# Where the transfers, measures and hashes of the first pairs stand, and a weight chunk behind stores, in a hashed attention followed by a feed-forward block

## The chip, the cores and the metric

The kernel runs on one core of a Trainium2 chip. The metric is the device time of one execution in microseconds, as the median of several executions; lower is better. The core has five instruction streams that run side by side and wait for each other by semaphores: TensorE (PE, matmuls), VectorE (DVE), ScalarE (ACT), GpSimd (POOL) and SyncE (SP, which here only issues DMA transfers). Each of them works through its own instructions in order. ScalarE also issues some transfers; an issue that waits holds up what stands behind it on ScalarE.

## The reference: what is computed

Attention in which a query sees only the keys in its hash bucket, then a two-layer block with a sigmoid gate. q, k and v have the shape (4, 8, 768, 64).

```python
q_bits = (np.einsum('bhsd,dk->bhsk', q, proj) > 0)
k_bits = (np.einsum('bhsd,dk->bhsk', k, proj) > 0)
mask = q_bucket[:, :, :, None] == k_bucket[:, :, None, :]
scores = np.where(mask, scale * np.matmul(q, k.transpose(0, 1, 3, 2)), -1e9)
attn = softmax(scores)
x = np.matmul(attn, v)                # to (3072, 512)
h = x @ w_in                          # 512 x 2048
g = h * (1.0 / (1.0 + np.exp(-1.702 * h)))
out = g @ w_out                       # 2048 x 512
```

## The kernel before, in words

**Pairs.** The 4 x 8 heads are worked through two at a time, as 16 pairs (`pairs`, pair 0 to pair 15). The two heads of a pair fill the 128 partitions. The order of instructions on the four computing engines is the order of the program text (`manual_schedule`, `ORDERED`); SyncE's transfers keep the order of the program through `load`. Nothing here is put in order by a planner.

**What a pair needs.** `fetch(n, "k")` and `fetch(n, "q")` issue four transfers each on SyncE and bring k and q in blocks of 32; `turn` transposes them on VectorE into the tile `own`; `exchange` copies `own` to `other` with the 32-row halves swapped (four transfers on SyncE). `measure` sums the squares of k or q on ScalarE (for a guard at the end; the result isn't used before then), and it reads the tile that `fetch` wrote, as `turn` does. That tile is shared: `fetch(2, name)` writes where pair 0's was, `fetch(3, name)` where pair 1's was, and each waits for the `turn` and the `measure` of the earlier pair. `fetch_v` brings v in one transfer.

**Features.** `hashed(n, at)` multiplies with the hash vectors on TensorE into a PSUM tile; `featured(n)` makes of it signed 0/1 features `f` on VectorE (one instruction) and then spreads `f` over the tile `feats[n % 2]` with eight small transfers of 16 rows (12 KB each). They go out on SyncE, except for two of pair 1 (q, first half), which ScalarE issues. From pair 2 on, `copied` makes a second copy of the features with two more transfers, since `scores_of_four` works on 32-row blocks. The features add a large number to the score where buckets agree, so they stand in the same PSUM sum as the product of q and k; scores of a pair can't begin without them.

**A pair's stream.** `scores` or `scores_of_four` fills PSUM tiles with scores for 128 keys; `weigh` takes the exponential on ScalarE into `es[0]` or `es[1]` (first and second half of the queries). `values` multiplies with v, and `unload` brings the result to `xT` on ScalarE. `add_low` (GpSimd) and `add_high` (VectorE) add the exponentials over the keys; `total` finishes these sums over partitions on TensorE, `invert` and `norm` turn them on VectorE into a factor and scale `xT` by it. In the loop over n = 2 to 15 the second half of pair n-1 and the first half of pair n go side by side, with `invert` and `norm` of pair n-2.

**PSUM tiles.** There are four places of two banks each. `in_turn()` gives them out one after the other by the counter `turns`; a tile waits until the one four turns before it in the same place has been read. Pair 0 takes its places from the written list `slots` and from `place(3)`.

**The row of transfers.** Every transfer of SyncE or ScalarE gets one of eight semaphores, in turn, along one row that the framework lays out; it waits until the transfer eight places before it in the row has landed. So a transfer's place in the row decides whom it waits for, also across the two issuers. `behind_issue(dma, other)` puts a transfer behind another one in the row without making it wait for it.

**Feed-forward.** Weights come in chunks of 512 KB (`convert`: one transfer, then six steps on VectorE and one on ScalarE). The two last chunks of w_in (`late`) are converted after the attention by `conversions`; the first is issued on SyncE right after `hidden(0, 0)`, the first output block, and its first step on VectorE stands in `hidden(0, 1)`. The products use a scheme with seven products in place of eight, nested: `sums_a` and `sums_b` make sums of operands, for a good part on GpSimd (lines 217 to 228), and `keep` stores the gated results to `g_dram`, 256 KB at a time at first; GpSimd's sums of results (`outer_sums`, `g_outer`) overwrite tiles that `keep` is storing, and wait for that.

Of the kernel before, what the change touches and what calls it, by code (L numbers as in the profile page):

```python
# [38 lines left out]
def kernel(  # L39
# [113 lines left out]


# [134 lines left out]
    def attention(ff):  # L289
# [4 lines left out]
        with actx:  # L294
# [47 lines left out]
            def behind_issue(dma, other):  # L342

                tc.add_manual_dep(dma.ins, other.ins.name,
                                  mybir.DependencyInfo(mybir.DependencyClass.NoSync, mybir.DependencyReason.DATA), reason="row")

# [26 lines left out]
            def first_pair():  # L373
# [48 lines left out]
                placed("q", tq, 1, (act, dve))  # L422

# [12 lines left out]
            def exchange(n):  # L436

                for j in range(2):
                    for i in range(2):
                        r0, r1 = D * j + 32 * i, D * j + 32 * (1 - i)  # L440
                        load(other[n % 3][r0 : r0 + 32], own[n % 3][r1 : r1 + 32])
# [19 lines left out]
            def featured(n):  # L461
# [3 lines left out]
                for c in range(2):  # L465
                    for i, x in enumerate("kq"):

                        for j in range(2):
                            r0 = D * i + 32 * c + 16 * j
                            to, of = feats[n % 2][x][D * j : D * j + 16, c * HS : (c + 1) * HS], f[r0 : r0 + 16, :]  # L470
                            if (n, x, c) == (1, "q", 0):
                                nc.scalar.dma_start(out=to, in_=of)
# [143 lines left out]
            fetch_v(0)  # L616
            slots = [2, 0, 1] * 5
            scores(0, 0, low, slots)
            measure(0, "k")
            fetch(2, "k")  # L620
# [10 lines left out]
            fetch_v(1)  # L631
# [5 lines left out]
            values(0, 0, high, at[:, 0])  # L637
            hashed(1, at[:, 1])
            unload(0, 0)
            whole(featured(1))  # L640
            scores(0, 1, high, slots)
# [3 lines left out]
            exchange(2)  # L645
# [24 lines left out]
            next(inverse[0])  # L670
            scores_of_four(1, ((1, 0), (1, 2), (1, 4)))
            add_low(1, 1)
            norm(0)
            add_high(1, 0, (2,))
            for x in "kq":
                measure(3, x)
            at = in_turn()
            values(1, 0, every, at[:, 0])
            hashed(3, at[:, 1])
            unload(1, 0)  # L680
            for n in range(2, last + 1):

                more = n + 2 <= last
                if n == last:

                    turns[0] += 1
# [828 lines left out]
```

## Time and profile before

| | |
|---|---|
| three runs | 859.0, 858.53, 859.93 us (median 859.0) |
| the profiled execution | 857.87 us; span from first to last instruction 856.1 us |
| mean granted TensorE clock | 0.996 |
| TensorE / weight loads | 98% / 61% busy |
| VectorE / ScalarE / GpSimd | 79% / 39% / 43% busy |
| moved by DMA | 144.92 MB, mean 169 GB/s |

How to read the lines: a timeline row has the start and the duration in us, the engine, the line of the kernel, the operation and its tiles (written <- read), how many such instructions are merged, and in square brackets how long the engine had been idle before and who released it. SPq and ACTq are the issuing of transfers by SyncE and ScalarE; the duration there holds the waits between merged issues. A row of a stretch gives the stretch, its length, then busy time and count of TensorE, its weight loads, VectorE, ScalarE and GpSimd, then the granted TensorE clock, the mean busy share of the DMA engines and GB/s. A row of waits gives the total in us, the number and the longest.

### The profile page before, as it was taken

The page shows a single profiled execution, that of the slowest core. Times are in us where ns is not written, and L with a number is a line of the kernel's source. Part 1 is how long each engine was busy: PE and PEld are TensorE (multiplying, and loading weights), DVE is VectorE, ACT ScalarE, POOL GpSimd, SP SyncE. Part 2 cuts the span into 40 slices and gives each one's busy share as a digit, 9 for nine tenths or more (in the row PEclk, how much of TensorE's full clock was granted, in tenths as well). Part 3 has the DMA queues.
Part 4 walks back from the last instruction along what each step waited for, and adds up shares of the span by engine and source line. Part 5 has one row for each costly group of instructions (what it writes and reads, how often), then busy time and mean ns, then how long its engine had stood idle before and what let it go on. Part 6 is the DMA issues. An engine that isn't in the chain of part 4 may idle for free.

```text
span 856.1 us, 14954 instructions
## 1 busy us (share of the span) xinstructions
PE 841.2 (98%) x5644; PEld 522.2 (61%) x5644; DVE 672.1 (79%) x1068; ACT 337.5 (39%) x552; POOL 364.8 (43%) x321
## 2 busy tenths in 40 slices
PE   9989999999999999999999999999999999999996
PEld 4534444444444444565666666545888888888885
DVE  5558788888878986787887788676998977897776
ACT  6746667667666544333444444433000000000000
POOL 4314334434343438997854466668664100000000
PEclk9999999999999999999999999999999999999999
DMA  8476767676674204435566636577854675467524
GB/s 146 86 152 148 153 150 158 129 148 150 143 159 105 72 1 136 159 115 230 198 221 221 221 148 230 187 259 279 286 167 156 205 248 190 162 211 243 191 109 100
DMA packets 165197, 144.92 MB, mean 169 GB/s; under 512 B 124224, under 2 KB 139712, under 8 KB 159872
## 3 DMA queue, kind: packets, MB, share of 16 engines
q1 hardware_dynamic: 154640, 112.11, 46.9%
q10 hardware_dynamic: 10480, 31.81, 11.1%
q8 instruction: 45, 0.74, 0.3%
q14 instruction: 32, 0.26, 0.1%
HBM read 79.69 MB, written 50.33 MB: 152 GB/s over the span
## 4 chain that ended last, share of the span: by engine, by line
PE 87%; POOL 6%; DVE 2%; ACT 1%; issue 1%; DMA 1%; SPq 0%; ACTq 0%; DVEq 0%; POOLq 0%
PE product L1238 30%; PE product L911 16%; PE s L512 15%; PE s L545 14%; PE small L979 5%; PE product L979 2%; PE s L494 2%; PE s L458 1%; PE s L567 1%; ACT e L482 1%; DMA g_dram<-u 1%; POOL c L227 1%; POOL v L226 1%; POOL u L225 1%; POOL w_in_sb L218 0%
## 5 line engine op out<-in xcount | busy, mean ns | idle before, releaser
L482 ACT ACTIVATE e<-s 128x768 f32<-128x768 f32 x192 | 143.3, 812 | 55.8 <-PE s L512 49.1
L545 PE MATMUL s<-e,v 128*32 128x385 f32 x1536 | 131.1, 488 | 0.0
L523 POOL TENSOR_TENSOR t_x<-e 128x768 f32<-128x768 f32 x32 | 59.2, 1849 | 145.6 <-ACT e L482 145.6
L911 PE MATMUL product<-xT,w_in_sb 128*128 128x512 f32 x216 | 100.0, 593 | 0.1
L545 PEld LDWEIGHTS s<-e,v 128*32 128x32 f32 x1536 | 46.6, 109 | 79.3 <-issue 62.0
L911 PE MATMUL product<-t_x,s_in 128*128 128x512 f32 x192 | 89.5, 593 | 1.3 <-ACT u L1033 1.3
L512 PE MATMUL s<-s_in 32*128 32x384 f32 x912 | 89.3, 488 | 0.0
L523 POOL TENSOR_TENSOR t_x<-t_x,e 128x768 f32<-128x768 f32 x32 | 54.6, 1705 | 43.8 <-ACT e L482 42.4
L1274 ACT COPY u<-product 128x256 f32<-128x256 f32 x20 | 7.4, 372 | 158.1 <-PE product L1238 124.9
L536 DVE TENSOR_TENSOR acc<-acc,e 128x768 f32<-128x768 f32 x63 | 67.8, 1076 | 2.1
L911 PEld LDWEIGHTS product<-xT,w_in_sb 128*128 128x128 f32 x216 | 40.9, 190 | 35.8 <-issue 32.7
L512 PEld LDWEIGHTS s<-s_in 32*128 32x128 f32 x912 | 44.8, 187 | 23.7 <-issue 2.9
L911 PEld LDWEIGHTS product<-t_x,s_in 128*128 128x128 f32 x192 | 36.4, 190 | 31.3 <-issue 27.3
L512 PE MATMUL s<-own 32*128 32x384 f32 x432 | 44.3, 482 | 0.0
L463 DVE TENSOR_SCALAR f<-s,above,weight 128x384 bf16<-128x384 f32 x15 | 10.1, 676 | 41.5 <-PE s L567 30.3
L927 DVE TENSOR_TENSOR u<-product,u 128x256 f32<-128x256 f32 (+1 forms) x60 | 28.3, 485 | 15.6 <-PE product L979 12.9
L533 DVE SCALAR_TENSOR_TENSOR acc<-t_x,e 128x768 f32<-128x768 f32 x31 | 29.3, 947 | 11.4 <-POOL t_x L523 10.8
L1238 PE MATMUL product<-raw_g,xT 128*128 128x256 f32 x152 | 35.1, 379 | 0.0
L512 PE MATMUL s<-feat 32*128 32x384 bf16 x336 | 29.8, 327 | 3.8 <-DMA feat<-feat 3.3
L512 PEld LDWEIGHTS <-feat 32*128 32x128 bf16 x336 | 10.3, 92 | 38.1 <-issue 26.2
L225 POOL TENSOR_TENSOR u<-v,u 128x1024 f32<-128x1024 f32 (+1 forms) x11 | 23.8, 2168 | 22.4 <-ACT v L924 14.5
L226 POOL TENSOR_TENSOR v<-c,v 128x1024 f32<-128x1024 f32 (+1 forms) x15 | 32.4, 2158 | 1.0
(297 smaller groups left out, 1781.0 us busy)
## 6 DMA issues: line engine op xcount, KB each, us to landing
raw_g<-g_dram SPq DMA_DIRECT2D x20, 1024.0 KB, 5.1
s_in<-g_dram SPq DMA_DIRECT2D x20, 1024.0 KB, 5.1
g_dram<-c ACTq DMA_DIRECT2D x18, 512.0 KB, 2.9
raw<-in_moe_w_out_dram ACTq DMA_DIRECT2D x16, 512.0 KB, 3.6
raw<-in_moe_w_in_dram ACTq DMA_DIRECT2D x15, 512.0 KB, 3.8
s_in<-own SPq DMA_DIRECT2D x36, 192.0 KB, 4.0
v<-in_v_dram SPq DMA_DIRECT2D x16, 384.0 KB, 4.0
k<-in_k_dram SPq DMA_DIRECT2D x52, 96.0 KB, 3.0
```

Of the source, the lines that this page charges most:

```text
L225: return [lambda: eng.tensor_tensor(t1, b12, b11, op=Alu.subtract), lambda: eng.tensor_tensor(b12, b22, b12, op=Alu.subtract), lambda: eng ...
L226: lambda: eng.tensor_tensor(b12, b22, b12, op=Alu.subtract),
L482: nc.scalar.activation(es[c][:, kt, :, 0:HS], ps[:, :, 0:HS], Act.Exp, scale=1.0 / D**0.5)
L512: nc.tensor.matmul(ps[i][:, j, 0:HS], a[r0 : r0 + 32, keys], m[r0 : r0 + 32, cols], start=at == 0, stop=at == 2)
L523: nc.gpsimd.tensor_tensor(low_sum, low_sum if i else e[:, 0], e[:, i + 1], op=Alu.add)
L533: nc.vector.scalar_tensor_tensor(acc, terms[0], T * TINY, terms[1], op0=Alu.add, op1=Alu.add)
L536: nc.vector.tensor_tensor(acc, acc, terms[i + 1], op=Alu.add)
L545: nc.tensor.matmul(av[D * j + d : D * j + d + 32, :], vt[:, j, row, d : d + 32], es[c][:, t, j, :], start=(t == 0), stop=(t == T - 1))
L911: nc.tensor.matmul(ps, wq[LEFT[i]][:, kc, :], xq[RIGHT[i]][:, kc, :], start=(start and kc == 0), stop=(kc == K2 - 1), skip_group_check=not ...
L927: nc.vector.tensor_tensor(dst, x, y, op=Alu.add)
L979: nc.tensor.matmul(x, wq[LEFT[i]], xq[RIGHT[i]], start=start, stop=True, skip_group_check=True)
L1238: nc.tensor.matmul(ps, wq[LEFT[i]][:, c, :], gq[RIGHT[i]][:, c, :], start=(onto is None and c == 0), stop=(c == F4 - 1), skip_group_check= ...
```

## The change

1. `featured` gets an argument `behind`; the two transfers that ScalarE issues for pair 1 stand in the row behind the last transfer of `exchange(2)`. `exchange` returns that transfer, and `behind_issue` moves to where both blocks see it.
2. Pair 0 to 3, other places: `measure(0, "k")` right behind the turns of pair 0; `fetch(2, "k")` ahead of the first scores; `turn(2)`, `measure(2)` and `exchange(2)` ahead of the features of pair 1; `fetch_v(1)` behind these features; `fetch(4, "q")` behind `copied(2)`.
3. `hashed(1)` and `hashed(2)` take a place of their own from `slots`, not the second half of the tile of `values`. `values(1, 0)` and `hashed(3)` take two turns instead of one; `total(0)` shares the tile of `hashed(3)`, behind pair 1's scores, not ahead of them.
4. `invert(0)` and `norm(0)` move into the loop's turn n = 2, which treats n = 2 like the others; the loop's extra `turns[0] += 1` at n = 15 goes.
5. The first late chunk stands in the row behind the third store of `hidden(0, 0)`.

```diff
@@ first_pair @@
                 placed("q", tq, 1, (act, dve))
+                measure(0, "k")
@@ exchange @@
-                        load(other[n % 3][r0 : r0 + 32], own[n % 3][r1 : r1 + 32])
+                        dma = load(other[n % 3][r0 : r0 + 32], own[n % 3][r1 : r1 + 32])
+                return dma
@@ featured @@
-            def featured(n):
+            def featured(n, behind=None):
...
                             if (n, x, c) == (1, "q", 0):
-                                nc.scalar.dma_start(out=to, in_=of)
+                                behind_issue(nc.scalar.dma_start(out=to, in_=of), behind)
@@ attention @@
             fetch_v(0)
+            fetch(2, "k")
             slots = [2, 0, 1] * 5
             scores(0, 0, low, slots)
-            measure(0, "k")
-            fetch(2, "k")
...
             values(0, 0, low, at[:, 0])
-            fetch_v(1)
...
             add_low(0, 1)
-            values(0, 0, high, at[:, 0])
-            hashed(1, at[:, 1])
-            unload(0, 0)
-            whole(featured(1))
-            scores(0, 1, high, slots)
             for x in "kq":
                 turn(2, x)
                 measure(2, x)
-            exchange(2)
+            values(0, 0, high, at[:, 0])
+            hashed(1, place(slots.pop(0))[:, 0])
+            unload(0, 0)
+            behind = exchange(2)
+            whole(featured(1, behind))
+            fetch_v(1)
+            scores(0, 1, high, slots)
             add_high(0, 1)
             at = place(3)
             values(0, 1, every, at[:, 0])
-            hashed(2, at[:, 1])
+            hashed(2, place(slots.pop(0))[:, 0])
             unload(0, 1)
-            at = place(0)
-            total(0, at[:, 0])
             turns[0] = 1
-            features = featured(2)
-            next(features)
-            inverse = {0: invert(0)}
-            next(inverse[0])
-            whole(features)
-            for x in "kq":
-                fetch(4, x)
+            whole(featured(2))
+            fetch(4, "k")
...
             copied(2)
+            fetch(4, "q")
...
-            next(inverse[0])
...
-            norm(0)
...
+            values(1, 0, every, in_turn()[:, 0])
             at = in_turn()
-            values(1, 0, every, at[:, 0])
-            hashed(3, at[:, 1])
+            hashed(3, at[:, 0])
+            total(0, at[:, 1])
             unload(1, 0)
+            inverse = {}
             for n in range(2, last + 1):
-                if n == last:
-                    turns[0] += 1
...
-                if n > 2:
-                    inverse[n - 2] = invert(n - 2)
-                    next(inverse[n - 2])
-                    step(n - 1, 2 if n == last else 1)
+                inverse[n - 2] = invert(n - 2)
+                next(inverse[n - 2])
+                step(n - 1, 2 if n == last else 1)
@@ feed_forward, keep and conversions @@
-                (queue or loader[0]).dma_start(out=dst, in_=x)
+                stored.append((queue or loader[0]).dma_start(out=dst, in_=x))
...
-                next(gens[0])
+                dma = next(gens[0])
+                if late:
+                    behind_issue(dma, stored[2])
```

More of the change, by code (lines that the diff above doesn't have):

```diff
@@ L152, with behind_issue @@
     CW = 512
+    def behind_issue(dma, other):
+        tc.add_manual_dep(dma.ins, other.ins.name,
+                          mybir.DependencyInfo(mybir.DependencyClass.NoSync, mybir.DependencyReason.DATA), reason="row")
     masks = {}
@@ L340, in load @@
                 return tc.keep_in_program_order(nc.sync.dma_start(out=out, in_=in_))
-            def behind_issue(dma, other):
-                tc.add_manual_dep(dma.ins, other.ins.name,
-                                  mybir.DependencyInfo(mybir.DependencyClass.NoSync, mybir.DependencyReason.DATA), reason="row")
             def fetch(n, name):
@@ L704, in attention @@
                 add_low(n, 0)
-                if n > 2:
-                    next(inverse[n - 2])
+                next(inverse[n - 2])
                 if more:
@@ L713, in attention @@
                 add_high(n - 1, 1, (2,))
-                if n > 2:
-                    norm(n - 2)
+                norm(n - 2)
                 if more:
@@ L920, in keep @@
                     dst = dst.rearrange("p m (k t) -> p m k t", k=x.shape[2])
-                (queue or loader[0]).dma_start(out=dst, in_=x)
+                stored.append((queue or loader[0]).dma_start(out=dst, in_=x))
+            stored = []
             def emit(c, of=None):
```

## The prediction

> **What bounds the kernel now.** I read the page first, then the waits of TensorE alone, then the busy time by stretches, then the timelines around each gap, and last the chain that ended last.
>
> ```profile
> span 856.1 us, 14954 instructions
> PE 841.2 (98%) x5644; PEld 522.2 (61%) x5644; DVE 672.1 (79%) x1068; ACT 337.5 (39%) x552; POOL 364.8 (43%) x321
> ...
> 0.00:70.00 70.00, 63.70 (x573) 31.03 (x577) 38.74 (x62) 44.08 (x73) 25.42 (x69) 0.98 0.71 132
> ...
> 840.00:856.10 16.10, 9.33 (x44) 7.87 (x42) 8.65 (x17) 0.37 (x1) 0.00 (x0) 0.88 0.58 132
> ```
>
> TensorE (PE) is busy for 841.2 of 856.1 us. Of the 14.9 us in which it is not, 6.3 lie in the first 70 us and 6.8 in the last 16, which the change does not touch. So the change can only win inside the few waits that the view of TensorE's waits names, each shown at its place below: 3.33, 1.27, 0.98 and 0.36 us. It takes no matmul away, so I price each wait, and ask whether a new one comes.
>
> **The two waits of the first pairs.** Here is TensorE around them, with two rows of a later, undisturbed iteration and two of the chain of waits for the period.
>
> ```profile
> 30.10 1.09 PE L567 MATMUL s<-acc,ones 128*32 128x384 f32 x8
> 32.17 0.44 PE L494 MATMUL s<-feat 64*128 64x384 bf16 x2 [0.98 <-issue]
> 46.74 0.34 PE L512 MATMUL s<-feat 32*128 32x384 bf16 x2
> 50.40 0.98 PE L512 MATMUL s<-feat 32*128 32x384 bf16 x2 [3.33 <-DMA feat<-feat]
> 50.89 2.95 PE L512 MATMUL s<-s_in 32*128 32x384 f32 x16
> 59.42 1.46 PE L512 MATMUL s<-s_in 32*128 32x384 f32 x16
> 69.97 0.83 PE L567 MATMUL s<-acc,ones 128*32 128x384 f32 x8
> 70.73 0.34 PE L512 MATMUL s<-feat 32*128 32x384 bf16 x4
> ...
> 70.80 3.02 PE s L512 x40
> 89.32 3.02 PE s L512 x40
> ...
> 50.00:60.00 10.00, 9.60 (x98) 4.89 (x102) 3.09 (x5) 4.34 (x8) 3.23 (x2) 0.83 0.74 184
> ```
>
> Scores of pair 1 begin at 32.17 after 0.98 us of nothing. Pair 2 begins at 46.74 and stops 3.33 us for the copies of its features. Behind that stop sixteen matmuls take 2.95 us that take 1.46 at 59.42, and the granted clock of that stretch is 0.83: the wait is paid once as idleness and again as slow matmuls. The Trainium skill (TensorE: Matmul & The Clock Gate, Part 1) says that the gate halves the clock after an idle window of about 3.4 us, and that the window runs free of the kernel. The trace agrees with the halving, at a gap of 3.33 us; whether it strikes in every execution is a rival below.
>
> With TensorE never waiting: the sums of pair 0 (`total(0)`, at 30.10) move behind pair 1, so scores of pair 1 can begin at 30.10. They and what follows take 46.74 - 32.17 = 14.57 us, the moved sums 70.73 - 69.97 = 0.76. Pair 2 would begin at 45.43. One period is 89.32 - 70.80 = 18.52, so pair 3 begins at 63.95 and not 70.73: **6.78 us**, of which 0.98 + 3.33 are the waits and 2.47 the slow clock (2.14) and the sums' slower end (1.09 against 0.76).
>
> **Why they wait: the SyncE queue.** In the built kernels each transfer of SyncE and ScalarE takes one of eight semaphores in its turn, and waits until the transfer eight places ahead has landed.
>
> ```profile
> 19.35 7.79 SPq L340 DMA_DIRECT2D xT<-in_k_dram  x4
> 24.24 0.68 DVE L463 TENSOR_SCALAR f<-s,above,weight 128x384 bf16<-128x384 f32 x1 [5.45 <-ACT xT L557]
> 25.00 1.25 ACTq L472 DMA_DIRECT2D feat<-f  x2
> 29.71 3.74 SPq L340 DMA_DIRECT2D feat<-f  x6
> 36.72 5.36 SPq L340 DMA_DIRECT2D feat<-f  x8
> 42.19 2.23 SPq L340 DMA_DIRECT2D k<-in_k_dram  x4
> 44.51 3.55 SPq L340 DMA_DIRECT2D q<-in_q_dram  x4
> 48.10 1.16 SPq L340 DMA_DIRECT2D feat<-feat  x2
> ...
> SPq L340 <- DMA feat<-f: 5.4, 2, 5.2
> ```
>
> ScalarE's two transfers of pair 1 stand in the row among the loads of pair 2, though they can only start at 25.00. So the load of pair 3 that begins at 19.35 sticks for 5.2 us, and every later transfer of SyncE is late by that. The edit `behind_issue` puts the two behind the exchange. To follow SyncE in the changed order I use these rows too:
>
> ```profile
> 9.80 2.47 ACT L482 ACTIVATE e<-s 128x768 f32<-128x768 f32 x3 [1.81 <-PE s L494]
> 13.11 2.03 SPq L340 DMA_DIRECT2D k<-in_k_dram  x4
> 16.77 2.02 DVE L536 TENSOR_TENSOR acc<-acc,e 128x768 f32<-128x768 f32 x2
> 17.28 0.84 ACT L448 ACTIVATE xT<-xT 128x768 f32<-128x768 f32 x1
> 22.50 0.49 PE L458 MATMUL s<-own,pf_q 128*32 128x384 f32 x2
> 23.06 0.16 ACT L556 COPY vs<-s 128x1 f32<-128x1 f32 x1 [1.94 <-PE s L458]
> 42.56 2.42 DVE L588 TENSOR_TENSOR xT<-xT,rs 128x768 f32<-128x768 f32 x1
> 67.45 2.59 SPq L340 DMA_DIRECT2D s_in<-own  x4
> ...
> k<-in_k_dram SPq DMA_DIRECT2D x52, 96.0 KB, 3.0
> ```
>
> - `measure(0, "k")` goes into ScalarE's 1.81 us of idleness ahead of 9.80 and costs nothing (without that cover it would push the exponentials back by the 0.84 of the measure at 17.28). It frees the buffer of the four loads `fetch(2, "k")` at about 9 and not 13.11. Those of q wait for the next measure, behind the exponentials (9.80 + 2.47 + 0.84, so 13.2): they are issued by 15.3 and landed near 18.3, at the 3.0 us of the last row.
> - The eight loads of pair 3 wait for ScalarE's measures of pair 1, the last of which ends at 18.1; they need two times 2.03, so they are issued by about 21.5 (an estimate, without the hole) and not by 29.71.
> - `turn(2)` and its two measures now come ahead of the features of pair 1. VectorE is free at 18.8 (16.77 + 2.02); its two transposes end at 20.6. ScalarE's two measures take 2 x 0.84 of the 1.94 us of idleness ahead of its unload at 23.06. The exchange's four transfers go out from 21.5 to 24.1 (2.59).
> - Hashes of pair 1 end at 23.0 (22.50 + 0.49) in a bank of their own, so the features need not wait for the unload in the shared tile: about 23.1 to 23.8 on VectorE, not 24.24. Two transfers of SyncE at 24.1 and 24.7, ScalarE's two at 24.3 to 25.5. The needed four land by 27.5 even at the 2.3 us that the copies take today (48.10 to 50.40), against 30.10: margin 2.6 us. The bank they take is wanted by the third scores tile, at about 24.6; margin 0.8.
> - `fetch_v(1)`, one transfer, moves behind these features, to about 28; wanted at 40.0 (values of pair 1).
> - Features of pair 2: hashed by 30.1, on VectorE to about 31, eight transfers to 36.4 (5.36), `fetch(4, "k")` to 38.6 (2.23), the two copies to 39.8 (1.16) and, with 2.3 more from the second's start near 39.2, landed by 41.5. They are wanted at 45.43: margin 3.9 us. Putting `fetch(4, "q")` behind them is 3.55 of that.
> - `invert(0)` and `norm(0)` move into the loop's first turn, which was without them. The norm of pair 0 takes 2.42. VectorE is busy for 3.09 of the ten us from 50 on, so some 5 us fit; without that cover they would delay sums that free the second half of the exponentials, with about 3 us to spare.
>
> Bounds of this part: 6.78 above. From below, if the copies landed so late that all 3.33 and the slow clock stayed, only 0.98 to 1.3 would be won. I take 6.78, since both margins on landings are 2.6 us or more.
>
> **The skipped bank.** The changed program uses one more tile for pair 1 (`values(1, 0)` and the hashes of pair 3 apart), and drops the skip `turns[0] += 1` in the last pair.
>
> ```profile
> 292.51 0.34 PE L512 MATMUL s<-feat 32*128 32x384 bf16 x2
> 293.21 0.34 PE L512 MATMUL s<-feat 32*128 32x384 bf16 x2 [0.36 <-ACT e L482]
> ```
>
> The last pair's second tile falls, because of the skip, on the bank whose exponential had only just ended. Without the skip it falls on one freed a tile earlier. The second pair of matmuls would come at about 292.7, not 293.21: **0.5 us**, between 0 and 0.5.
>
> **The chunk behind the stores.**
>
> ```profile
> 328.60 0.32 SPq L921 DMA_DIRECT2D g_dram<-u  x1
> 330.83 0.63 ACT L924 ACTIVATE v<-v 128x512 f32<-128x512 f32 x1 [1.77 <-DVE v L927]
> 333.89 1.26 POOL L225 TENSOR_TENSOR u<-v,u 128x512 f32<-128x512 f32 x1 [3.47 <-DMA g_dram<-u]
> 387.65 1.98 PE L911 MATMUL product<-t_x,s_in 128*128 128x512 f32 x4 [1.27 <-ACT u L1033]
> ...
> g_dram<-u SPq DMA_DIRECT2D x2, 256.0 KB, 2.6
> ```
>
> GpSimd waits 3.47 us until the store of `u`, issued at 328.60, has landed (5.2 us), then works without a gap until TensorE waits 1.27 us for it at 387.65. Ahead of that store in the same queue stands a load of 512 KB; the later stores of `u` land in 2.6. Behind three stores the load delays none of them. The start then lies between 331.46 (330.83 + 0.63) and 333.89, a lead of 0 to 2.4 us; I take a landing of 3 us, so a lead of about 2.3. More than 1.27 is enough: **1.27 us**. The Trainium skill (DMA: Bandwidth & Descriptors, Queues, rings and completion order) says that one issuer's descriptors are consumed in ring order on each DMA engine; by it the load's transfer time comes off, by a fixed cost of writing to memory alone it would not. The 5.2 against 2.6 agrees with the first.
>
> **Sum.** 6.78 + 0.5 + 1.27 = 8.55. The profiled execution took 857.87 (its span and 1.8 around it), so 849.3 by its own time; it lies 1.1 below the median of the three runs, 859.0. On that median: **850.5 us**.
>
> **Rivals.**
> 1. *The late part gives nothing* (load and stores overlap differently, another wait of GpSimd takes over): 6.78 + 0 to 0.5, about 852. For it: GpSimd is full from 334 to 387. Against: the margin.
> 2. *A stall of the front remains*: the features of pair 1 or the copies come 1 to 3 us after need. 852 to 855. For it: my chain of issues has ten links.
> 3. *The clock is not cut in the timed runs of before*, so its 2.1 us are not there to win: 852.6. It is what a free window would allow at a gap this near its length. Against: the median is above the profiled time, not below it.
> 4. *The edit of the row does not free SyncE*, because pair 3's loads stick on something else: only the 1.8 of the two later parts and the move of `fetch(4, "q")` are left, 854 to 858.
> 5. *Slower*: ScalarE's two transfers sit in its order ahead of the exponentials of pair 0, and now hang on VectorE's `turn(2, "q")`, so on the load of q. If that load lands after about 23, the exponentials, the values of pair 0 and all of TensorE slip with it, one for one, and a gap over 3.3 us adds the slow clock's 2.1. To eat the 8.55 and end slower it must land after about 30. I have it landing near 18.3; against it stands that distance, for it only that ScalarE and VectorE wait in order.
>
> **How the numbers follow.** All three parts as summed: 0.60, 849.2 to 851.8. Rival 1: 0.12; rival 2: 0.13; rival 3: 0.04; rival 4: 0.05; rival 5: 0.06. The range 849.0 to 854.5 holds the first, the next, the fourth and most of rival 2. About 0.2% (1.7 us) is what a measurement of this kernel tells from no change; rivals 1 to 3 are faster by more, rival 4 half of the time not. So 0.91 faster, 0.03 same, 0.06 slower.
>
> **What would show it.** In the changed profile: no wait of TensorE for copies of features, and granted clock 1.00 in every stretch up to 840; SyncE's loads of pair 3 with no 5 us hole, ended by about 22; the copies for pair 2 issued near 39; pair 3 begun near 64; no 0.36 at the last pair's start; the store of `u` landing in about 3 us and no wait for ScalarE's `u` after 60 us of GpSimd. It is wrong if a new wait of more than 1 us stands in the first 70 us, or if the chunk's later load makes VectorE wait at its first use.

## The result, and the profile after

| | before | after |
|---|---|---|
| median of the timed runs | 859.46 us (858.53 to 860.17, 4 runs) | 848.83 us (848.73 to 849.19, 4 runs) |
| profiled execution | 857.87 us, span 856.1 | 848.73 us, span 846.9 |
| mean granted clock of the profiled execution | 0.996 | 0.999 |

The ratio of the times is 0.9878, 95% interval 0.9861 to 0.9895. The profiled executions differ by 9.14 us; the forecast sum was 8.55. The medians differ by 10.6. The median after lies 1.7 below the forecast of 850.5 and 0.17 below the lower end of the range.

The page of the kernel after: span, busy time by engine, and the chain of work that ended last by engine.

```profile
span 846.9 us, 14955 instructions
PE 838.0 (99%) x5644; PEld 519.2 (61%) x5644; DVE 673.8 (80%) x1068; ACT 337.6 (40%) x552; POOL 366.6 (43%) x321
...
PE 98%; POOL 1%; DVE 1%; ACT 0%; issue 0%; ACTq 0%; POOLq 0%; DVEq 0%
```

The first 70 us of the kernel after in the view of stretches (length, then busy time of PE, PEld, DVE, ACT and POOL, then granted clock, DMA share, GB/s):

```profile
0.00:70.00 70.00, 67.85 (x657) 31.25 (x661) 44.27 (x74) 48.72 (x80) 29.90 (x71) 1.00 0.79 148
```

In the first 70 us TensorE is busy for 67.85, where it was 63.70, and the clock there is 1.00 in place of 0.98. Its waits in the whole kernel (total us, times, longest) are the first few of the start-up and no others:

```profile
PE s L391 <- DVE idle L76: 1.3, 1, 1.3
PE s L410 <- POOL above L339: 0.4, 1, 0.4
PE s L410 <- ACT own L405: 0.2, 1, 0.2
PE s L400 <- DMA k<-in_k_dram: 0.2, 1, 0.2
```

The waits of 0.98, 3.33, 0.36 and 1.27 us that the prediction priced are all gone. TensorE's timeline after (start, us, then the instruction; no brackets means no idle time ahead of it), at the starts of pairs 1 and 2:

```profile
30.26 0.34 PE L496 MATMUL s<-feat 64*128 64x384 bf16 x2
...
44.60 0.83 PE L569 MATMUL s<-acc,ones 128*32 128x384 f32 x8
45.37 0.34 PE L514 MATMUL s<-feat 32*128 32x384 bf16 x4
```

Pair 2 begins at 45.37 (forecast 45.43) and pair 3 one period of 18.52 later, at 63.89 (forecast 63.95), against 70.73: 6.84 us won by there. SyncE's own queue, which the prediction had followed issue by issue, with ScalarE's two transfers from that engine's timeline:

```profile
17.32 2.42 SPq L345 DMA_DIRECT2D xT<-in_k_dram  x4
19.84 2.19 SPq L345 DMA_DIRECT2D xT<-in_q_dram  x4
22.13 2.59 SPq L345 DMA_DIRECT2D s_in<-s_in  x4
24.84 4.33 SPq L345 DMA_DIRECT2D feat<-f  x6
29.21 0.58 SPq L345 DMA_DIRECT2D v<-in_v_dram  x1
...
38.57 1.14 SPq L345 DMA_DIRECT2D feat<-feat  x2
```

```profile
23.86 1.76 ACTq L474 DMA_DIRECT2D feat<-f  x2
```

The loads of pair 3 (17.32 to 22.03) have no hole; before they sat at 19.35 to 29.60 (those of q end at 27.48 + 2.12) with 5.2 us of waiting inside. The copies for pair 2 go out at 38.57 and not 48.10, 6.8 us ahead of the pair. The granted clock is 1.00 in every stretch up to 840 us. The other two parts of the sum show in two places. Between the sums before the last pair and those behind it lie 14.94 us, where it was 15.64. First before, then after:

```profile
291.52 0.85 PE L567 MATMUL s<-acc,ones 128*32 128x384 f32 x8
307.16 0.83 PE L567 MATMUL s<-acc,ones 128*32 128x384 f32 x8
...
284.67 0.85 PE L569 MATMUL s<-acc,ones 128*32 128x384 f32 x8
299.61 0.83 PE L569 MATMUL s<-acc,ones 128*32 128x384 f32 x8
```

And GpSimd's first product on `u` no longer waits for the store, which left SyncE at 321.07 and so had landed in under 2.9 us:

```profile
323.99 1.27 POOL L230 TENSOR_TENSOR u<-v,u 128x512 f32<-128x512 f32 x1 [1.10 <-ACT v L915]
```

TensorE's matmuls on both sides of the place where it waited 1.27 us for `u` (387.65 in before), first before, then after:

```profile
385.78 0.60 PE L979 MATMUL small<-w_out_sb,w 128*128 128x256 f32 x2
389.47 0.59 PE L979 MATMUL small<-xT,w 128*128 128x256 f32 x2
...
378.24 0.59 PE L970 MATMUL small<-w_out_sb,w 128*128 128x256 f32 x2
378.67 1.88 PE L900 MATMUL product<-t_x,s_in 128*128 128x512 f32 x4
380.38 0.59 PE L970 MATMUL small<-xT,w 128*128 128x256 f32 x2
```

### The profile page after: what moved, and what is told of

Read it like the earlier page. It is cut to its first block, busy times and chain, and to the rows that moved or that the text cites. A ratio compares the mean times of both kernels' runs of the same rounds, so it can differ in the third digit from the quotient of the medians.

```text
span 846.9 us, 14955 instructions
## 1 busy us (share of the span) xinstructions
PE 838.0 (99%) x5644; PEld 519.2 (61%) x5644; DVE 673.8 (80%) x1068; ACT 337.6 (40%) x552; POOL 366.6 (43%) x321
## 4 chain that ended last, share of the span: by engine, by line
PE 98%; POOL 1%; DVE 1%; ACT 0%; issue 0%; ACTq 0%; POOLq 0%; DVEq 0%
PE product L1229 30%; PE product L900 23%; PE s L547 15%; PE s L514 15%; PE small L970 6%; PE product L970 3%; PE s L496 2%; PE s L460 1%; PE s L569 1%; PE s L410 0%; POOL feat L337 0%; DVE feat L411 0%; ACT c L915 0%; DVE own L405 0%; DVE v L918 0%
## 5 line engine op out<-in xcount | busy, mean ns | idle before, releaser
L538 DVE TENSOR_TENSOR acc<-acc,e 128x768 f32<-128x768 f32 x63 | 70.1, 1112 | 2.3
L465 DVE TENSOR_SCALAR f<-s,above,weight 128x384 bf16<-128x384 f32 x15 | 10.2, 677 | 39.8 <-PE s L569 33.9
L1229 PE MATMUL product<-raw_g,xT 128*128 128x256 f32 x152 | 35.1, 379 | 0.0
L918 DVE TENSOR_TENSOR v<-product,v 128x512 f32<-128x512 f32 x24 | 16.5, 688 | 20.0 <-PE product L900 20.0
L1229 PEld LDWEIGHTS product<-raw_g,xT 128*128 128x128 f32 x152 | 28.9, 190 | 3.9
```

The lines of the kernel that those rows point to most:

```text
L538: nc.vector.tensor_tensor(acc, acc, terms[i + 1], op=Alu.add)
L918: nc.vector.tensor_tensor(dst, x, y, op=Alu.add)
L1229: nc.tensor.matmul(ps, wq[LEFT[i]][:, c, :], gq[RIGHT[i]][:, c, :], start=(onto is None and c == 0), stop=(c == F4 - 1), skip_group_check= ...
```

## The experiments

All medians below stand beside runs of the kernel before on the same chip: 859.21 in the session of copies_first, chunk_only, no_skip and row_undone, 859.59 in that of fill_the_stop, row_and_copies, stop_put_back and chunk_undone, 860.05 in that of q_first, measure_back and row_alone. The ratios are to these; the median of after, 848.83, comes from a session of its own (before: 859.46). A table at the end of this section brings them together.

**copies_first.** Before, with the load of q of pair 4 behind the copies of pair 2, and nothing else.

```diff
-            for x in "kq":
-                fetch(4, x)
+            fetch(4, "k")
...
             copied(2)
+            fetch(4, "q")
```

> The kernel before with one edit: the loads of q for pair 4 stand behind the two copies of pair 2's features. Theory 1 (the stop of TensorE at pair 2 is the copies' place in SyncE's queue): the copies are issued near 44.5 and landed near 47; the stop shrinks from 3.33 us to under 0.7 and the slow clock behind it goes; the profiled execution takes about 853 (857.9 less 4.9). Theory 2 (the 1.1 to 1.6 us by which the timed runs of before exceed its profiled execution belong to that stop and the clock cut behind it, which vary from execution to execution): the median lies within 0.4 of the profiled time and the runs within 0.6 of each other. Rival (the excess has another place): the median stays 1 us or more above the profiled time, about 854.2.

855.02 us, ratio 0.9953 [0.9939, 0.9966]. The stop at pair 2 is gone, yet the time is 2 us above the expected 853, and the runs spread over 2.6 us. Pair 3 begins at 66.21, which is 4.5 earlier than before, but the next five periods take 18.61, 19.14, 19.10, 19.03 and 18.94 and not 18.52: 2.2 us are given back. The timeline of this kernel, all engines, in the second of them:

```profile
95.96 0.70 DVE L181 SCALAR_TENSOR_TENSOR w_in_sb<-raw,mask_3fffffff 128x512 uint32<-128x512 uint32 x1 [1.53 <-DMA raw<-in_moe_w_in_dram]
...
98.76 0.69 ACT L193 ACTIVATE raw<-raw 128x512 f32<-128x512 f32 x1 [2.20 <-DVE bits L185]
...
100.34 0.58 ACT L557 ACTIVATE xT<-s,vs 128x384 f32<-128x384 f32 x1
...
100.98 0.34 PE L512 MATMUL s<-feat 32*128 32x384 bf16 x2 [0.30 <-ACT xT L557]
```

The chunk of weights in the row lands late, VectorE waits 1.53 us for it, ScalarE waits 2.20 for VectorE, its unload (L557) is late by that, and TensorE finds the bank of its next scores tile still taken. The tile starts 0.6 us late in this period. The next three long periods lose their time elsewhere: there the four matmuls that open a pair take 0.57 to 0.88 us and not 0.34, and the trace does not name what they wait for. So SyncE's 5 us hole in the row, still there in this kernel, is not only the cause of the stop. Where no stop takes its place, the lateness stays in the loop and is paid in small parts.

**row_alone and row_and_copies.** The first is before with the edit of the row alone, which also moves the turns, measures and exchange of pair 2 ahead of the features of pair 1; the second is that with the edit of copies_first as well.

```diff
-            whole(featured(1))
-            scores(0, 1, high, slots)
             for x in "kq":
                 turn(2, x)
                 measure(2, x)
-            exchange(2)
+            behind = exchange(2)
+            whole(featured(1, behind))
+            scores(0, 1, high, slots)
...
-                                nc.scalar.dma_start(out=to, in_=of)
+                                behind_issue(nc.scalar.dma_start(out=to, in_=of), behind)
```

> The kernel of row_and_copies with the load of q of pair 4 back ahead of the copies: before with the edit of the row alone. Theory (either of the two edits takes the stop of pair 2 away, the row by making SyncE's queue 3 to 5 us earlier, the copies by taking 3.55 us from ahead of them; only the row also takes the lateness that copies_first paid for): copies issued near 44 to 45, landed near 47.5, wanted at 47.7; a stop of 0 to 0.6 us, granted clock 1.00, periods 18.5; 852.5 to 854.2. Rival (the stop needs both edits): a stop of 2 us or more, 855 to 858.

> The kernel before with the copies of pair 2 ahead of the load of q of pair 4 (as in copies_first, 855.0) and besides the edit of the row: turns, measures and exchange of pair 2 ahead of the features of pair 1, ScalarE's two transfers behind that exchange. Sums, banks, the late load of v and the skip stay as before. Theory (copies_first gave 2.3 us back in the periods of pairs 3 to 7 because SyncE's queue ran late by its hole of 5 us in the row): loads of pair 3 without the hole, periods of 18.5 throughout, pair 3 at 65.3 to 66.2; 851.5 to 853.0. Rival (those periods are long for another reason: the norm of pair 0, the chunk in the row, the banks): 854.3 to 855.2.

row_alone: 853.40 us, ratio 0.9917 [0.9898, 0.9936]. row_and_copies: 853.06 us, ratio 0.9930 [0.9917, 0.9944]; just above its range of 851.5 to 853.0, while its profiled execution took 851.78. Both have periods of 18.5 throughout. In the profiled execution of row_alone, the slowest of its six runs at 855.34, the copies still come a little late, by more than the 0.6 us expected at most:

```profile
47.92 0.34 PE L513 MATMUL s<-feat 32*128 32x384 bf16 x3
49.39 0.33 PE L513 MATMUL s<-feat 32*128 32x384 bf16 x1 [1.13 <-DMA feat<-feat]
```

The granted clock is 1.00 on both sides of this 1.13 us. So the row alone shortens the stop to one that costs no clock, and the copies' move takes the rest. By TensorE's start behind the stop the copies land only 1.0 us earlier than in before (49.39 against 50.40); the other half of the shrinking is that TensorE reaches pair 2 later, 47.92 against 46.74. It is later because the edit of the row alone makes a new wait. First ScalarE's timeline, then TensorE's, in row_alone:

```profile
27.16 1.43 ACTq L473 DMA_DIRECT2D feat<-f  x2
28.64 2.22 ACT L483 ACTIVATE e<-s 128x768 f32<-128x768 f32 x3 [2.55 <-DMA xT<-in_q_dram]
```

```profile
29.50 2.26 PE L546 MATMUL s<-e,v 128*32 128x385 f32 x24 [1.62 <-ACT e L483]
```

ScalarE's two transfers now wait for the load of q of pair 3 and hold up the exponentials of pair 0 behind them, and TensorE waits 1.62 us for these (1.13 in row_and_copies). In after the loads of pair 3 stand 2.3 us earlier (17.32 against 19.64 here), the transfers leave at 23.86, and there is no such wait.

In the median the row alone wins 860.05 - 853.40 = 6.65 in its own session, where copies_first won 4.19, and both edits together 6.53, no more than the row alone. The parts do not add up: each of the two edits takes the same stop. In the profiled executions the row wins less, 857.87 - 855.34 = 2.53, with 855.34 the slowest of its runs.

**row_undone.** The reverse: after, with ScalarE's two transfers in their old place in the row.

```diff
-                                behind_issue(nc.scalar.dma_start(out=to, in_=of), behind)
+                                nc.scalar.dma_start(out=to, in_=of)
```

> The changed kernel with one edit undone: ScalarE's two transfers of pair 1 are not put behind the exchange in the row. Now the exchange of pair 2 waits for them (issue near 25.7 and not 22.1), so the first transfers of pair 1's features land near 31 and TensorE waits 0.5 to 0.8 us at pair 1's scores; the copies of pair 2 still land 2 us ahead of need. Theory 1: 849.3 to 849.7 in profile and median. Rival (the edit of the row carries the front part): the stop at pair 2 returns in part, 851 or more.

850.88 us, ratio 0.9902 [0.9888, 0.9916], over 1 us more than expected. SyncE's exchange of pair 2 and TensorE's scores of pair 1:

```profile
25.87 2.48 SPq L345 DMA_DIRECT2D s_in<-s_in  x4
```

```profile
31.71 0.50 PE L496 MATMUL s<-feat 64*128 64x384 bf16 x2 [1.25 <-issue]
```

The exchange is 3.74 us later than after's 22.13, TensorE waits 1.25 at the scores of pair 1 (the trace names no releaser; it is where the features were expected to be late), and three of the later periods take 19.20, 18.79 and 18.92, which is 1.35 more than three of 18.52. The same late queue as in copies_first, with no stop at pair 2.

**measure_back and q_first.** After, with one of its other two moves in SyncE's row undone: the measure of pair 0's k and the loads that wait for it at their old place, or the load of q of pair 4 ahead of the copies.

```diff
-                measure(0, "k")
...
-            fetch(2, "k")
             slots = [2, 0, 1] * 5
             scores(0, 0, low, slots)
+            measure(0, "k")
+            fetch(2, "k")
```

> The kernel after with the measure of pair 0's k and the loads of pair 2's k that wait for it at their old places, behind the first exponentials and the load of v. Theory (the early measure gives SyncE some 2 us in the row, which is margin and no more): loads of pair 3 from about 19.4 instead of 17.32, exchange of pair 2 at 24 to 25.4 instead of 22.13, features of pair 1 landed by 29.5 and wanted at 30.3; 848.7 to 849.4. Rival (SyncE's lateness costs in proportion, as in row_undone, where 3.7 us of it cost 2.0): 849.6 to 850.6, with a wait at pair 1 or long periods for pairs 3 to 7.

```diff
-            fetch(4, "k")
+            for x in "kq":
+                fetch(4, x)
...
             copied(2)
-            fetch(4, "q")
```

> The kernel after with the load of q of pair 4 put back ahead of the copies of pair 2. Theory (the prediction's margin of 3.9 us at these copies, of which the move is worth 3.55; the rows of after show the copies at 38.57, so without the move they start near 41 and land near 43.5, wanted at 45.7): no stop, 848.6 to 849.2, runs within 0.7 us. Rival (the landing takes longer behind the load of q, as the 4.55 us of stop_put_back were more than the 1.5 to 3.3 expected): a stop of 1 to 3 us, 850 to 854.

measure_back: 849.74 us (849.31 to 850.17), ratio 0.9877 [0.9853, 0.9901], 0.9 above after. The loads of pair 3 go out at 18.93, the exchange at 23.66, and TensorE waits 0.38 us at pair 1; pair 3 begins at 64.62, 0.73 later than in after. The median lies between the two expectations: the move is margin for the most part, and a little time. Against before in its own session the ratio is 0.9877, where after has 0.9878, so the medians alone do not show the difference. q_first: 849.00 us (848.89 to 849.40), ratio 0.9866 [0.9842, 0.9890], no stop, with the copies issued at 41.47 and pair 2 begun 4.4 us later. With the row repaired the move of `fetch(4, "q")` was not needed, as the prediction's margin of 3.9 less 3.55 had it.

**fill_the_stop.** Before, with 13 matmuls of zeros inside the stop. They keep TensorE running and bring nothing else forward.

```diff
                             keys = slice((k0 + i) * P, (k0 + i + 1) * P)
+                            if (n, c, k0, at, i) == (2, 0, 0, 0, 1):
+                                for _ in range(13):
+                                    nc.tensor.matmul(ps[1][:, 0], idle[:, 0:P], idle, start=True, stop=True)
                             for j in range(2):
```

> The kernel before, with 13 matmuls of zeros (128x512, bf16; about 2.8 us by the 0.21 to 0.23 us of one at full clock, an estimate) put into TensorE's stop at the start of pair 2. They write a tile that the next matmul overwrites, so nothing of the result changes and the copies land no sooner. Theory (the stop costs its 3.33 us and, through the granted clock, about 2.1 more, and the length of the cut differs from run to run, which is why the median of before lies above its profiled time): the clock stays 1.00 behind the stop, the sixteen matmuls there take about 1.46 and not 2.95, pair 3 starts near 68.6 and not 70.73; 855.7 to 856.3 by the profiled time, and the runs lie within about 1 us of each other with a mean clock of .997 or more. Rival (the spread of before comes from something else, transfers say): the profiled time falls by 2 too, but the runs still spread over 2 us and more. Second rival (slow matmuls behind the stop are not due to idleness): 857.9 and more, nothing won.

856.54 us (855.68 to 858.14), ratio 0.9969 [0.9957, 0.9981]: faster by doing more. The profiled execution took 856.82, above the expected 855.7 to 856.3, and pair 3 starts at 69.85, not near 68.6. TensorE's timeline in this kernel:

```profile
47.54 0.34 PE L515 MATMUL s<-feat 32*128 32x384 bf16 x2
47.80 2.98 PE L512 MATMUL s<-idle 128*128 128x512 bf16 x13
50.72 0.33 PE L515 MATMUL s<-feat 32*128 32x384 bf16 x1
51.34 0.33 PE L515 MATMUL s<-feat 32*128 32x384 bf16 x1 [0.29 <-DMA feat<-feat]
51.34 1.62 PE L515 MATMUL s<-s_in 32*128 32x384 f32 x16
```

The stretch from 50 to 60 us of the same kernel:

```profile
50.00:60.00 10.00, 9.71 (x117) 4.70 (x118) 4.46 (x7) 4.50 (x8) 3.23 (x2) 1.00 0.80 188
```

The copies still come after 3 us, but the sixteen matmuls behind them take 1.62 us and not 2.95, and the clock of the stretch is 1.00 and not 0.83. The slow matmuls were the price of idleness, and no property of the data that came late. The profiled execution won only 1.05 us against that of before, since in it TensorE came to pair 2 0.8 us later and the copies landed 0.9 us later. The runs still spread over 2.5 us, as the rival said, though their mean clock is .997 to .999 throughout. So the clock is at most one part of the spread of before, and not all of it.

**stop_put_back.** After, with the copies of pair 2 moved late, so that the stop returns in an otherwise changed kernel.

```diff
-            copied(2)
             fetch(4, "q")
             for x in "kq":
                 turn(3, x)
             fetch_v(2)
             exchange(3)
+            copied(2)
```

> The kernel after with the copies of pair 2 put behind the load of q of pair 4, the load of v and the exchange of pair 3 in SyncE's queue. By the rows of after they are then issued at about 45 to 46 and land at 47 to 49, where TensorE wants them at 45.7: a stop of 1.5 to 3.3 us. Theory (a stop near 3.3 us cuts the clock, a shorter one doesn't, and only then do the runs spread): if the stop is under 3, 850.3 to 851.8 with a clock of .998 and runs within 0.7 us; if it is longer, 853 to 855 with a clock of .995 or .996 and runs spread over 2 us. Rival (the spread comes from elsewhere in before): runs within 0.7 us in either case.

856.20 us (855.54 to 857.71), ratio 0.9964 [0.9950, 0.9978]. The stop is longer than expected, the cut comes with it, and the time lies above the 853 to 855 expected for that case. First TensorE's timeline, then the stretch from 50 to 60 us of this kernel:

```profile
50.26 0.69 PE L514 MATMUL s<-feat 32*128 32x384 bf16 x2 [4.55 <-DMA feat<-feat]
50.45 3.06 PE L514 MATMUL s<-s_in 32*128 32x384 f32 x16
```

```profile
50.00:60.00 10.00, 9.74 (x102) 5.24 (x106) 5.49 (x6) 4.59 (x8) 3.23 (x2) 0.83 0.35 83
```

Up to the sums of pair 0, at 44.61, this kernel runs as after does to 0.01 us; those of pair 1 stand at 69.67 and not 63.12, 6.55 later: 4.55 of stop and 2.00 of slow clock. Three of its six runs had a mean clock of .996 or .997 and took 855.5 to 855.7; the other three had .994 and took 856.7 to 857.7. By these clocks the cut is not the same length in every execution, and a longer one goes with 1 to 2 us more. That is inferred from the mean clock: in the profiled executions that have the cut it lasts 3.4 us each time, here and in before. The stretch in before:

```profile
50.20:53.60 3.40, 3.20 (x18) 1.94 (x22) 1.74 (x3) 0.00 (x0) 0.00 (x0) 0.50 1.03 233
```

**no_skip.** Before, with the skip of a bank at the last pair removed and the count of tiles moved by one in its place.

```diff
-            turns[0] = 1
+            turns[0] = 2
...
-                if n == last:
-
-                    turns[0] += 1
```

> The kernel before without the skipped turn in the last pair (the count starts one later, so the last pair has the same places). Theory 1: both small waits at the start of the last pair go, 0.70 us between the last pair's predecessor and its second group: profiled near 857.2, median near 858.7 by theory 2. Rival: only the second tile's wait goes, 0.36 to 0.5 us.

857.37 us, ratio 0.9977 [0.9968, 0.9985]. The period of the last pair takes 14.94 in place of 15.64 us, so 0.70, the same as in after. The rest of the 1.84 us by which its median lies below that of before is not in that place: the profiled execution also passed through the feed-forward block 1.17 us faster, where nothing was edited (the store below landed earlier). The start of that pair in TensorE's timeline:

```profile
292.43 0.85 PE L567 MATMUL s<-acc,ones 128*32 128x384 f32 x8
293.21 0.54 PE L512 MATMUL s<-feat 32*128 32x384 bf16 x4
293.42 0.98 PE L512 MATMUL s<-own 32*128 32x384 f32 x8
```

**chunk_only and chunk_undone.** The chunk's edit put into before, and taken out of after.

```diff
-                next(gens[0])
+                dma = next(gens[0])
+                if late:
+                    behind_issue(dma, stored[2])
```

> The kernel before with one edit: the first late chunk stands in the row behind the third store. Theory 1: the store of u lands in under 3 us, GpSimd starts about 2 us earlier, the 1.27 us wait of TensorE goes and 1.3 to 1.6 us with it: profiled near 856.4. Theory 2: the excess of the timed runs stays, median near 857.8 with a spread over 1 us. Rival: the excess belongs to the contention of chunk and stores, and the median lies within 0.4 of the profiled time.

> The kernel after without the edit of the chunk (its load stands in its old place in the queue, ahead of the three stores). Theory (the edit won 1.54 us of the profiled 9.1, and no_skip showed that the store can land earlier by itself): 849.4 to 850.4, with a spread of over 0.7 us between runs and a wait of TensorE for ScalarE's u of up to 1.3 us. Rival (with the first part 7.5 us earlier the store no longer meets the load): 848.6 to 849.1, no such wait.

chunk_only: 857.83 us, ratio 0.9986 [0.9978, 0.9995], 1.4 less than before in its session. Its profiled execution took 857.83 too, not the expected 856.4: the wait of TensorE for ScalarE's `u` is gone and the feed-forward block 1.14 us shorter, but pair 3 began 1.16 us later than in before. chunk_undone: 849.33 us (848.76 to 849.60), ratio 0.9884 [0.9868, 0.9899], 0.5 more than after, which is hardly clear of noise: the ranges of the runs overlap, and the two come from different sessions. In its trace GpSimd still waits for the store, but less, and TensorE does not wait for ScalarE's `u`:

```profile
324.47 1.27 POOL L230 TENSOR_TENSOR u<-v,u 128x512 f32<-128x512 f32 x1 [1.54 <-DMA g_dram<-u]
```

Counted from the start of the feed-forward block, this product begins at 17.72 us in before, at 16.48 in no_skip, which does not have the edit either, at 15.80 in chunk_undone, at 15.93 in chunk_only, which has it, and at 15.36 in after. What the edit is worth depends on how late the store happens to land.

**All of them.** The margin is the time from SyncE's issue of a pair's copies to the first matmul of that pair; the smallest is that of pairs 2 to 7. TensorE's waits are those between 20 us and the last pair. Margins, waits and the cut are those of the one profiled execution. The spread is that of 4 to 6 runs, except for before. no_skip and chunk_only (11 runs each) keep the stop of before and its cut and spread over 2.2 and 1.9 us.

| kernel | median us | spread of its runs, us | margin at pair 2 | smallest margin | TensorE's waits, us | clock cut |
|---|---|---|---|---|---|---|
| after | 848.83 | 0.46 | 6.8 | 6.8 | none | no |
| q_first | 849.00 | 0.51 | 4.4 | 4.4 | none | no |
| chunk_undone | 849.33 | 0.84 | 6.7 | 6.1 | none | no |
| measure_back | 849.74 | 0.86 | 6.2 | 5.5 | 0.38 | no |
| row_undone | 850.88 | 1.41 | 5.3 | 2.4 | 1.25 | no |
| row_and_copies | 853.06 | 2.11 | 6.1 | 4.1 | 1.13 | no |
| row_alone | 853.40 | 2.56 | stop of 1.13 | stop | 1.62, 1.13 | no |
| copies_first | 855.02 | 2.58 | 3.2 | 2.3 | 1.40, 0.30 | no |
| stop_put_back | 856.20 | 2.17 | stop of 4.55 | stop | 4.55 | yes |
| fill_the_stop | 856.54 | 2.46 | stop, filled | stop | 1.25, 0.29 | no |
| before | 859.21 | 3.23 (23 runs) | stop of 3.33 | stop | 0.98, 3.33 | yes |

## Why the prediction was right or wrong

**The two waits of the first pairs: right, 6.78 forecast, 6.84 measured.** The chain of issues held to within some 0.7 us at each link. Loads of pair 3 issued by about 21.5: 22.03. Exchange 21.5 to 24.1: 22.13 to 24.72. SyncE's first features of pair 1 at 24.1: 24.84. Copies of pair 2 to 39.8: 39.71. That the stop is paid twice was shown by fill_the_stop, which took away the second payment alone, and by stop_put_back, which brought back both. The Trainium skill (TensorE: Matmul & The Clock Gate, Part 1) has the clock halved after an idle window of about 3.4 us that runs free of the kernel. The runs agree as far as they go: no cut at gaps of 1.13 to 1.62 us, and at 3.33 and 4.55 a clock of 0.50 for 3.4 us. That the window runs free of the kernel no run here shows.

**Why SyncE was late: right.** The prediction tied the hole to ScalarE's two transfers. row_undone shows it from one side: with the two in their old place the exchange stands 3.74 us later. row_alone shows it from the other: the loads of pair 3 end at 26.00 and not 29.60, and the stop shrinks to 1.13 us, though about half of that comes from TensorE getting there later. What the prediction did not see is that a late queue costs time without any stop too (copies_first and row_undone). In before the stop hid this, because behind it every later pair had its copies 8.5 us and more ahead. The change did not run into it since it repairs the queue, so it cost the forecast nothing; the expectations of copies_first and row_undone missed by it.

**The skipped bank: right in kind, 0.5 forecast, 0.70 measured**, in no_skip and in after alike. The forecast counted the step from 292.7 to 293.21, that is only the second pair of matmuls. The first pair stood late as well: they began 0.99 us behind the start of the sums at 291.52, and in after 0.78.

**The chunk behind the stores: right in kind, 1.27 forecast, 1.54 in the two profiled executions.** The stretch from the start of the feed-forward block to the chain's next block at L1229 shrank from 279.34 to 277.80 us. The product on `u` began 2.36 earlier in it, where a lead of about 2.3 was forecast. All of the 1.54 lies at the one wait: from the matmuls at 385.78 to those at 389.47 it was 3.69 us, and in after from 378.24 to 380.38 2.14. The term was mis-sized because the idle time in brackets runs only from the end of the matmuls at 385.78, 0.60 after their start, where without a wait the next begins 0.43 after it (378.24 to 378.67); the four behind the wait took 1.82 and not 1.71 besides. Starts compared with starts give the whole price. But the term is no constant: 1.4 when put into before, 0.5 when taken out of after. The forecast took the 5.2 us of one store in one execution for the rule. In chunk_undone the product waited only until 3.4 us after the store's issue, with the load ahead of it all the same, and in chunk_only, with the load behind it, until 3.3 us. So the runs do not show that the place of the load alone sets the landing.

**The step that failed: "on that median".** The sum was made against the profiled execution, which gave 849.3. The prediction then added the 1.1 us by which that execution lay below the median of before, as if every kernel carried them, and so forecast 850.5. After's median lies 0.1 above its profiled time. The runs show that the difference is no constant of a kernel, and no property of the stop either: the profiled execution is one draw from runs that spread. In the twelve other kernels the median lies from 1.94 below the profiled time (row_alone) to 1.28 above it (row_and_copies, without a stop at pair 2). In chunk_only, which keeps the stop and its cut, the two are equal. Rival 3 leaned on the same difference ("the median is above the profiled time"); with one profiled execution against three runs its sign says little.

The added 1.1 also set the range. Its lower end of 849.0 left 0.3 below the sum that was made for the profiled execution, and with the bank and the chunk 0.47 larger than forecast that execution itself, at 848.73, fell below it. Of the miss of 1.7 us the added term makes 1.0; the bank (0.20), the chunk (0.27) and the front (0.06) make most of the rest.

**What stays open.** Why the runs of some kernels spread over 1.4 to 3.2 us and those of others over less than 0.9. The clock cut is a part of it at most. In the 23 runs of before in the first session, the three with a mean clock of .994 average 860.3 us, the eleven with .996 or .997 858.7; but small differences of the mean clock say little, since q_first, without a cut in its profiled execution, shows .997 to .999. fill_the_stop spreads over 2.5 us at a full clock. Two readings of the table fit, and no run tells them apart. One is the margin of the copies: 4.4 us or more where the runs lie close together, 4.1 or less where they don't. The other is TensorE's own waits near the start: 0.38 us or none where they lie close, 1.1 and more where they don't. The jitter of landings could come through either way, but no run shows the landings of a timed execution. Nor was it tried which of the transfers ahead of the store in the feed-forward block makes its landing vary from 3.4 to 5.6 us.

**The rivals.** None came in after. Rival 1 is refuted by the 0.70 and 1.54 us in its profile, rival 2 by its waits, rival 4 by its queue and by row_alone. Against rival 3 stands the mean clock of the timed runs, .993 to .998 in before and .997 to .999 in fill_the_stop. For rival 5, ScalarE's two transfers left at 23.86 in the profile after, when the features that they carry had just been made (23.79); nothing of TensorE waited behind them. But the danger was real: in row_alone and row_and_copies these two transfers waited for a load, of pair 3 and not of pair 2, and TensorE lost 1.62 and 1.13 us to it.

## What to carry to other kernels

A gap between the profiled time and the median is not a constant of the program, since the profiled execution is one draw from the spread: make the sum against the execution that the rows come from, do not carry the gap over to the changed kernel, and let the range reach to both sides by the spread of the runs. Price a wait by comparing the starts on both sides of it, not by its idle time alone. Where a queue is late, find the transfer that it waits behind, and count the distance from each issue to its use over the next several iterations, since lateness without a visible stop is paid there in parts. A stop of TensorE of 3 us or more is to be priced with the slow matmuls behind it, and if it can't be removed, work that keeps TensorE busy in it can get a part of that back.

## What the runs showed that was not expected

- 13 matmuls that compute nothing, put into a stop, made the kernel 3.05 us faster in the median (859.59 to 856.54) and 1.05 in the profiled execution (857.87 to 856.82), with the clock at 1.00 behind the stop and not 0.50.
- A SyncE queue that runs 6 to 7 us later than usual against TensorE (margins of 2.3 to 3.8 us and not 9.5) stays late for five iterations and costs 0.1 to 0.6 us in each (copies_first); in the one followed above, VectorE, ScalarE and a PSUM bank stand between the late transfer and TensorE. At a margin of 4.1 us it cost nothing in the profiled execution.
- Moved alone, the two transfers of ScalarE held up the exponentials behind them, and TensorE waited 1.62 us at a place where it had not waited before (row_alone).
- The same store with the same load ahead of it, in kernels that differ only far from it, landed 3.4 us (chunk_undone) to 5.6 us (row_alone) after its issue, by the start of the product that waits for it.
